# Last head takes up the former head's row sums at its first key pair; even heads' bound steps spread 2, 3, 2, 3

## Chip, cores and metric

One core of a Trainium2 chip runs the whole program in one launch. The metric is device time in microseconds (us), lower is better. The kernel before takes 1926.5 us, the median of three runs (1925.24 to 1927.55).

## What is computed

A layer norm without weights, attention of 32 heads against a given key and value cache, and a SwiGLU feed-forward whose activated output gates the attention's result:

```python
xn = layernorm(x)                                  # x: 2048 x 640, bf16
q  = (xn @ wq) in 32 heads of 192                  # wq: 640 x 6144
p  = softmax(q @ k_cache^T * 192**-0.5)            # 2048 keys for each head
s  = (p @ v_cache, heads joined) @ wo              # wo: 6144 x 640
g  = silu((silu(xn @ w1) * (xn @ w3)) @ w2)        # F = 1536
out = x + s * g
```

## The kernel before

The heads run one after the other. A head has four query blocks (`qb`) of 512 queries, and a block has eight key pairs (`p`, 0 to 7), each of two tiles of 128 keys. `step` (line 745) emits one pair: the scores matmuls of the pair into a PSUM tile `st` (L550, two such tiles exist, and the projection of the next head's queries takes its turn in them), the exponential on ACT (`weights`, L558) into the SBUF tile `pT`, and then some of the waiting value matmuls (`parts`), a few pairs behind the scores. At pair 1 of each block `extra` projects one block of queries of the next head (L355); in the last head, 31, it computes a piece of the feed-forward instead (`hidden_last`, whose two PSUM halves DVE casts to `gl` and `ul`, L952 and L953).

One `pT` tile holds two pairs, and the pool `pp` has three of them. So the tile that pairs 2 and 3 of a block write is the one that pairs 4 and 5 of the block before wrote.

Heads 2 to 30 (`in_quads`) multiply on 64x64 quarters of the array (L629), which leaves no room for a column of ones in the values, so DVE adds up the softmax's row sums (`row_sums`, all adds at L662): `fours` adds the two `pT` tiles of four pairs, twice in a block; `join` and `fold` add these up; `ends` makes the 128x512 tile `e` and has it turned by a DMA on SP's queue into `eT` (L688). `turned_sums` (L698 to L713, "the normalising" below) reduces `eT` to `rs`, takes the reciprocal, and scales the block's turned output `ox` into `ostage`. Before that `evict_quads` brings the block's output out of PSUM: ACT copies one half to `oa` (L653), DVE adds the other into `ot` (L654). Heads 0, 1 and 31 use 64x128 tiles with the ones column (L609) and need no such sums.

The sums are put off by a clock that counts pairs. `later(w, f)` lists a chore that is due `w` pairs on, and `do_chores` (line 720), the last act of each `step`, emits what is due. With the delays of the kernel the second `fours` of a block falls to pair 0 of the next block, `join`, `fold` and `ends` to its pair 2, and the normalising to pair 0 of the block after that. For head 30 the next blocks are those of head 31, and there `do_chores` returns at once at pairs 0 and 1.

`do_chores` also emits the list `lazy`: the steps by which an upper bound of the next head's scores is made, one at each pair in `slots`. Three key maxima (`fold_keys`, L407; the third also starts small copies on POOL), two sums of squares and the roots of them for the head's query weights (`column_lengths`, L428 and L434 to L442), and the bound itself (`head_bound`, DVE and one POOL reduction). An even head emits ten steps: seven for the next head, and the three of `column_lengths` for the head after that, which enter the list in the third block; an odd head emits four.

Nearly every instruction is pinned (`pin`): each engine takes its instructions in the order in which the program emits them. The tile framework adds the waits between engines and, for a tile of a pool, the wait for the last reader of the tile that had the space before.

Of the kernel before, what the change touches and what calls it, by code (L numbers as in the profile page):

```python
# [30 lines left out]
def _kernel_impl(ctx, tc, A_x, A_k_cache, A_v_cache, A_wq, A_wo, B_w1, B_w3, B_w2, out):  # L31
    nc = tc.nc
    _, SQ, D = A_x.shape
    _, H, SK, dh = A_k_cache.shape
# [5 lines left out]
    NQB = SQ // 512  # L40
# [109 lines left out]
    def in_quads(h):  # L150
        return 1 < h < H - 1
# [14 lines left out]
    with ExitStack() as actx:  # L166
# [491 lines left out]
        def later(wait, f, *a):  # L658
            chores.append((clock[0] + wait, f, a))

        def add(out, a, b):
            pin(nc.vector.tensor_tensor(out=out, in0=a, in1=b, op=ALU.add))  # L662

        def row_sums(hd, qb, p, w):
            sm = hd["sums"]

            def fours():
                t = aq["tree"].tile([P, 2, 1024], BF16, tag="tree", name="tree")
                a, b = sm["w"]
                sm["w"] = []  # L670
                add(t[:], a[:], b[:])
                sm["t"].append(t)

            def join():
                a, b = sm["t"]
                add(a[:], a[:], b[:])
                sm["t"].pop()

            def fold():
                t = sm["t"][0]  # L680
                add(t[:, 0, :], t[:, 0, :], t[:, 1, :])

            def ends():
                t = sm["t"].pop()[:, 0, :]
                e = aq["two"].tile([P, 512], BF16, tag="e", name="e")
                add(e[:], t[:, 0:512], t[:, 512:1024])
                eT = aq["two"].tile([P, 4, P], BF16, tag="eT", name="eT")
                pin(nc.sync.dma_start_transpose(out=eT[:], in_=e[:]))  # L688
                later(6, turned_sums, hd, qb, eT)

            sm["w"].append(w)
            if p % 4 == 3:
                later(2, fours)
            if p == NPAIR - 1:
                for f in (join, fold, ends):
                    later(4, f)
# [21 lines left out]
        aq = {}  # L718

        def do_chores(h, qb, p):  # L720
            if h == H - 1 and p < 2:
                return
            for c in [c for c in chores if c[0] <= clock[0]]:
                chores.remove(c)
                c[1](*c[2])
            slots = (5, 6, 7) if h % 2 == 0 or h == 1 else (5,)
            if p in slots and lazy and lazy[0][0] <= clock[0]:
                _, f, a = lazy.pop(0)
                f(*a)
# [15 lines left out]
        def step(hd, qb, p, extra=None):  # L745
            me = (hd["h"], qb)
            first = qb == 0 and p < 2
            st2 = scores(hd, qb, p, quads=before["quads"] if first else hd["quads"])
            old = [k for k, _ in parts if k != me]
            old_quads = bool(old) and heads_quads(old[0][0])  # L750
            if p == 1 and old_quads:
                while parts[0][0] != me:
                    next_part()
            pT2 = weights(st2, hd["nb"][qb], p)
            parts.extend((values_quads if hd["quads"] else values)(hd, qb, p, pT2))
            if hd["quads"] and p % 2 == 1:
                row_sums(hd, qb, p, acc["w"])
            if p == 0:
                while sum(k != me for k, _ in parts) > (2 if old_quads else 1):
                    next_part()  # L760
            elif p == 1:
                while parts[0][0] != me:
                    next_part()
            else:
                while len(parts) > (4 + (p > 2) if hd["quads"] else 3):
                    next_part()
            if extra:
                extra()
            while late:
                late.pop(0)()  # L770
            clock[0] += 1
            do_chores(hd["h"], qb, p)
# [129 lines left out]
        hx = fw.tile([P, SQ], BF16, name="hx")  # L902
        astack = ExitStack()
        fdp = astack.enter_context(tc.tile_pool(name="fdp", bufs=1, side="right"))
        for name, n in (("one", 1), ("two", 2), ("tree", 3)):
            aq[name] = astack.enter_context(tc.tile_pool(name=f"aq_{name}", bufs=n, side="right"))
        ffn_w_loads = [
            lambda: pin(nc.gpsimd.dma_start(out=w1_sb[:], in_=B_w1[:, FPIG + P:F].rearrange("(c p) f -> p c f", p=P))),
# [57 lines left out]
        for h in range(1, H):  # L966
# [10 lines left out]
            hd = heads[h]  # L977
# [11 lines left out]
            for qb in range(NQB):  # L989
                post = []  # L990
                if (h, qb) == (H - 1, 2):
                    while chores:
                        clock[0] += 1
                        do_chores(h, qb, 2)
                    astack.close()
                    acc["hTp"] = fstack.enter_context(tc.tile_pool(name="hTp", bufs=2, side="right"))
# [355 lines left out]
@with_exitstack  # L1352
def kernel(
    ctx: ExitStack,
    tc: tile.TileContext,
    A_x: bass.AP,
    A_k_cache: bass.AP,
    A_v_cache: bass.AP,
    A_wq: bass.AP,
    A_wo: bass.AP,  # L1360
    B_x: bass.AP,
    B_w1: bass.AP,
    B_w3: bass.AP,
    B_w2: bass.AP,
    out: bass.AP,
):
    _kernel_impl(ctx, tc, A_x, A_k_cache, A_v_cache, A_wq, A_wo, B_w1, B_w3, B_w2, out)
# [30 lines left out]
```

## Time and profile before

| | before |
|---|---|
| median of the runs | 1926.5 us (1925.24 to 1927.55) |
| the profiled execution | 1925.79 us |
| its span, first to last instruction | 1924.3 us |
| PE matmul busy | 1914.5 us (99%) |
| DVE, ACT, POOL busy | 1446.4 (75%), 1350.4 (70%), 600.3 us (31%) |
| granted TensorE clock, mean | 0.999 |

Times in the profile are microseconds from the first instruction of the profiled execution. A line of the timeline gives start, duration, engine, source line, operation, output<-inputs, and in brackets the idle time of the engine before it and what ended that. `xN` counts instructions merged into one line; the duration is then that of all. PE is the matmul unit, DVE the vector engine, ACT the scalar engine, POOL the general one, SP the one that starts most DMAs. Matmuls overlap, so the end of one lies after the start of the next.

### The profile page before, as it was taken

To read this page: it belongs to the slowest core of one execution; us is meant where nothing else is said; L and a number is where in the kernel's file an instruction comes from. 1 tells how busy PE (TensorE), PEld (TensorE's weight loads), DVE (VectorE), ACT (ScalarE), POOL (GpSimd) and SP (SyncE) were. 2 spreads that over 40 slices of the span, in tenths; PEclk is the share of its full clock that TensorE was granted. 3 is DMA by queue.
4 is the path that set the end of the run, shared out by engine and by line. 5 is a ranking of instruction groups with operands and counts; after the bars stand their busy time and mean duration, and the time that the engine had idled before them with its cause. 6 is when DMAs were issued, how large, how long until landed. Compare 5 with 4: busy or idle time off the path is not lost.

```text
span 1924.3 us, 75788 instructions
## 1 busy us (share of the span) xinstructions
PE 1914.5 (99%) x34631; PEld 1306.8 (68%) x34631; DVE 1446.4 (75%) x2326; ACT 1350.4 (70%) x1405; POOL 600.3 (31%) x757
## 2 busy tenths in 40 slices
PE   9999999999999999999999999999999999999999
PEld 5666667777777777777777777777777796454446
DVE  8668888888888888988888888888888875521111
ACT  7778888888888888888888888888888877210000
POOL 3433434343434333344333343433343320000000
PEclk9999999999999999999999999999999999999999
DMA  7714446444553455345544453446444523936763
GB/s 171 142 50 74 106 84 102 86 100 87 93 98 86 99 84 100 81 105 91 101 84 104 76 107 68 112 77 110 77 106 85 97 45 119 281 71 152 162 151 76
DMA packets 535684, 197.22 MB, mean 102 GB/s; under 512 B 486896, under 2 KB 528848, under 8 KB 535360
## 3 DMA queue, kind: packets, MB, share of 16 engines
q1 hardware_dynamic: 522416, 162.71, 43.5%
q0 software_dynamic: 8256, 24.58, 4.9%
q8 instruction: 271, 4.44, 1.0%
q10 hardware_dynamic: 4688, 5.05, 0.8%
q14 instruction: 53, 0.43, 0.1%
HBM read 54.26 MB, written 31.98 MB: 45 GB/s over the span
## 4 chain that ended last, share of the span: by engine, by line
PE 99%; SPq 0%; DVE 0%; ACT 0%; DMA 0%; POOL 0%; issue 0%; ACTq 0%
PE st L550 34%; PE obank L629 31%; PE ps L355 14%; PE ps_s L1142 8%; PE obank L609 3%; PE ps_s L1098 3%; PE ps_f L1162 2%; PE ps_gu L929 1%; PE ps_f L1178 1%; PE ps L340 0%; DMA KT<-in_A_k_cache_dram 0%; SPq L116 0%; PE ps_gu L340 0%; ACT pT L558 0%; SPq L100 0%; ACT xnT L283 0%
## 5 line engine op out<-in xcount | busy, mean ns | idle before, releaser
L558 ACT ACTIVATE pT<-st,nb 128x1024 bf16<-128x1024 f32 x1016 | 1124.6, 1113 | 182.0 <-PE st L550 151.6
L629 PE MATMUL obank<-pT,vt 64*64 64x256 bf16 (+1 forms) x14848 | 787.8, 323 | 0.0
L629 PEld LDWEIGHTS <-vt 64*64 64x64 bf16 x14848 | 499.7, 107 | 172.4 <-issue 1.9
L550 PE MATMUL st<-qS,KM 64*64 64x512 bf16 (+1 forms) x1951 | 416.7, 376 | 0.4 <-POOL qS L381 0.4
L550 PE MATMUL st<-qA,KT 64*64 64x512 bf16 (+1 forms) x1951 | 416.6, 376 | 0.0
L550 PE MATMUL st<-qD,KT 64*64 64x512 bf16 (+1 forms) x1951 | 416.6, 376 | 0.0
L550 PE MATMUL st<-qA,KM 64*64 64x512 bf16 (+1 forms) x1951 | 392.0, 376 | 0.0
L550 PE MATMUL st<-qS,KT 64*64 64x512 bf16 (+1 forms) x1951 | 391.9, 376 | 0.1
L550 PE MATMUL st<-qF,KT 64*64 64x512 bf16 (+1 forms) x1951 | 391.8, 376 | 0.0
L550 PEld LDWEIGHTS <-KT 64*64 64x64 bf16 (+1 forms) x7808 | 286.6, 107 | 129.8 <-issue 0.6
L381 POOL COPY qS<-qA 64x512 bf16<-64x512 bf16 x256 | 291.0, 1137 | 63.9 <-DVE qA L378 28.2
L662 DVE TENSOR_TENSOR tree<-pT,pT 128x2048 bf16<-128x2048 bf16 x232 | 299.7, 1292 | 1.6 <-ACT pT L558 1.6
L355 PE MATMUL ps<-xnT,wq 64*64 64x512 bf16 (+1 forms) x2390 | 291.8, 376 | 0.0
L355 PE MATMUL ps<-xnS,wq 64*64 64x512 bf16 (+1 forms) x2390 | 288.0, 376 | 0.0
L662 DVE TENSOR_TENSOR tree<-tree 128x2048 bf16<-128x2048 bf16 x232 | 265.8, 1146 | 4.0
L355 PEld LDWEIGHTS <-wq 64*64 64x64 bf16 (+1 forms) x4780 | 170.2, 107 | 74.7
L550 PEld LDWEIGHTS <-KM 64*64 64x64 bf16 (+1 forms) x3904 | 152.0, 106 | 54.8 <-issue 1.2
L385 POOL COPY qD<-qF 64x512 bf16<-64x512 bf16 x127 | 95.6, 753 | 292.1 <-ACT qF L378 288.2
L1142 PE MATMUL ps_s<-oT,wo_sb 128*128 128x512 bf16 x720 | 155.7, 379 | 0.0
L378 DVE CAST qA<-ps 128x512 bf16<-128x512 f32 x120 | 82.9, 691 | 95.2 <-ACT qF L378 94.6
L654 DVE TENSOR_TENSOR ot<-oa,obank 128x768 bf16<-128x768 f32 x116 | 110.1, 949 | 36.2 <-ACT oa L653 35.8
L653 ACT COPY oa<-obank 128x768 f32<-128x768 f32 x116 | 92.6, 798 | 62.8 <-PE obank L629 62.8
(159 smaller groups left out, 1628.8 us busy)
## 6 DMA issues: line engine op xcount, KB each, us to landing
o_scr<-ostage SPq DMA_DIRECT2D x64, 384.0 KB, 3.2
vt<-in_A_v_cache_dram SPq DMA_DIRECT2D x62, 384.0 KB, 4.9
wo_sb<-in_A_wo_dram POOLq DMA_DIRECT2D x1, 7680.0 KB, 30.6
wq<-in_A_wq_dram POOLq DMA_DIRECT2D x31, 160.0 KB, 4.2
hT_scr<-hblk SPq DMA_DIRECT2D x16, 256.0 KB, 2.9
xnS<-xnT POOLq DMA_DIRECT2D x8, 320.0 KB, 6.1
wq<-in_B_w_dram POOLq DMA_DIRECT2D x31, 80.0 KB, 3.7
wq<-in_A_wq_dram POOLq DMA_DIRECT2D x31, 80.0 KB, 3.3
```

The lines of the kernel that those rows point to most:

```text
L355: pin(nc.tensor.matmul(halves[t][c, :], lhsT=w[ROWS[t], s, c], rhs=xs[ROWS[t], s // 2, qs], start=(s == 0), stop=(s == 2 * DC - 1)))
L378: pin(c(out=dst[:, qs], in_=src))
L381: keep(nc.gpsimd.tensor_copy(out=qS[ROWS[t], qs], in_=qA[ROWS[1 - t], qs]))
L385: keep(copy(out=qD[:, qs], in_=qF[PGW:P, qs]))
L550: pin(nc.tensor.matmul(st2[c, t * 512:(t + 1) * 512], lhsT=k[:, c], rhs=q[ROWS[t], qs], start=(s == 0), stop=(s == 2)))
L558: pin(nc.scalar.activation(out=pT2, in_=st2[:], func=ACT.Exp, scale=SCALE, bias=nb[:]))
L609: pin(nc.tensor.matmul(acc["o"][b][:, r, (j % 2) * 256:(j % 2) * 256 + DH + 1], lhsT=pT2[ROWS[r], t * 512 + j * P:t * 512 + (j + 1) * P], ...
L629: pin(nc.tensor.matmul(acc["o"][r][ROWS[c], int(low), 0:n], lhsT=vt[ROWS[r], t, p, c0:c0 + DT], rhs=pT2[ROWS[r], t * 512 + q0:t * 512 + q0 ...
L653: pin(nc.scalar.copy(out=oa[:], in_=banks[0]))
L654: pin(nc.vector.tensor_tensor(out=ot[:], in0=oa[:], in1=banks[1], op=ALU.add))
L662: pin(nc.vector.tensor_tensor(out=out, in0=a, in1=b, op=ALU.add))
L1142: pin(nc.tensor.matmul(ps_of[d], lhsT=wo_sb[:, k, d * P:(d + 1) * P], rhs=part(k // KQ)[:, k % KQ, :], start=(k == 0), stop=(k == OC - 1)))
```

## The change

Three edits. In `do_chores` the last head no longer returns at pairs 0 and 1, so chores that are due there are emitted there. The normalising of head 30's last block gets a delay of 9 pairs in place of 6, and so falls to pair 3 of head 31's second block; it was at pair 2 of that block before, held up by the return. The slots of the even heads from 2 on are pairs 5 and 6 in the first and third block and 5, 6 and 7 in the second and fourth, where they were 5, 6 and 7 in all; since the list runs dry in the third block, where it was emitted 3, 3, 1, 3 it is now 2, 3, 2, 3. With that the third key maximum moves from the first block to the second, the roots from the second to the third, and the bound from pair 5 to pair 6 of the third block. The pool `tree` of the sums has two tiles in place of three.

```diff
                 pin(nc.sync.dma_start_transpose(out=eT[:], in_=e[:]))
-                later(6, turned_sums, hd, qb, eT)
+                later(6 if in_quads(hd["h"] + 1) or qb < NQB - 1 else 9, turned_sums, hd, qb, eT)
...
         def do_chores(h, qb, p):
-            if h == H - 1 and p < 2:
-                return
             for c in [c for c in chores if c[0] <= clock[0]]:
                 chores.remove(c)
                 c[1](*c[2])
-            slots = (5, 6, 7) if h % 2 == 0 or h == 1 else (5,)
+            slots = (5,) if h % 2 and h > 1 else (5, 6) if h > 1 and qb % 2 == 0 else (5, 6, 7)
...
-        for name, n in (("one", 1), ("two", 2), ("tree", 3)):
+        for name, n in (("one", 1), ("two", 2), ("tree", 2)):
```

## The prediction

> **What bounds the kernel now.** I read the page first, then who waited for whom, then the timelines of PE, ACT and DVE around PE's longest wait.
>
> ```profile
> span 1924.3 us, 75788 instructions
> ...
> PE 1914.5 (99%) x34631; PEld 1306.8 (68%) x34631; DVE 1446.4 (75%) x2326; ACT 1350.4 (70%) x1405; POOL 600.3 (31%) x757
> ...
> PE 99%; SPq 0%; DVE 0%; ACT 0%; DMA 0%; POOL 0%; issue 0%; ACTq 0%
> ```
>
> PE's matmuls are 99% of the span and of the chain that ended last. PE is without work for 1924.3 - 1914.5 = 9.8 us in all, and only there can a change of order gain. The view of waits says where (total, times, longest):
>
> ```profile
> PE obank L609 <- ACT pT L558: 3.1, 2, 2.9
> PE fill L217 <- DVE cols L182: 1.9, 1, 1.9
> PE st L550 <- POOL qS L381: 0.4, 1, 0.4
> PE ps L340 <- ACT xnT L283: 0.2, 1, 0.2
> ```
>
> The largest is one wait of 2.9 us for an exponential. PE's timeline places it at the start of head 31, where value matmuls are L609:
>
> ```profile
> 1584.34 0.38 PE L550 MATMUL st<-qF,KT 64*128 64x512 bf16 x1
> ...
> 1585.55 0.38 PE L550 MATMUL st<-qS,KM 64*128 64x512 bf16 x1
> ...
> 1586.20 0.50 PE L609 MATMUL obank<-vt,pT 64*128 64x193 bf16 x8
> 1589.58 0.51 PE L609 MATMUL obank<-vt,pT 64*128 64x193 bf16 x8 [2.88 <-ACT pT L558]
> 1589.92 0.38 PE L550 MATMUL st<-qS,KM 64*128 64x512 bf16 x1
> ...
> 1601.36 0.38 PE L550 MATMUL st<-qS,KM 64*128 64x512 bf16 x1
> ...
> 1602.67 0.38 PE L550 MATMUL st<-qS,KM 64*128 64x512 bf16 x1
> ```
>
> The first line ends the scores of pair 2 in head 31's first block, the second begins those of pair 3, the fifth those of pair 4: 1589.92 - 1585.55 = 4.37 us. The last two are the same pairs in its second block: 1602.67 - 1601.36 = 1.31 us. So the stall costs 4.37 - 1.31 = 3.06 us, a little more than the 2.88 of idle, since the last matmul's modelled tail counts as busy. ACT and DVE tell why:
>
> ```profile
> 1578.82 1.11 ACT L558 ACTIVATE pT<-st,nb 128x1024 bf16<-128x1024 f32 x1 [0.18 <-PE st L550]
> ...
> 1583.54 1.14 ACT L524 ACTIVATE pt<-qF 64x512 bf16<-64x512 bf16 x2
> 1588.41 2.12 ACT L558 ACTIVATE pT<-st,nb 128x1024 bf16<-128x1024 f32 x2 [3.73 <-DVE tree L662]
> ```
>
> ```profile
> 1575.60 1.21 DVE L662 TENSOR_TENSOR tree<-pT,pT 128x2048 bf16<-128x2048 bf16 x1
> 1582.67 0.95 DVE L654 TENSOR_TENSOR ot<-oa,obank 128x768 bf16<-128x768 f32 x1 [5.86 <-ACT oa L653]
> 1584.01 0.69 DVE L952 CAST gl<-ps 128x512 bf16<-128x512 f32 x1 [0.38 <-PE ps L355]
> 1584.61 0.68 DVE L953 CAST ul<-ps 128x512 bf16<-128x512 f32 x1
> 1585.21 0.68 DVE L702 TENSOR_REDUCE rs<-eT 128x4 f32<-128x512 bf16 x1
> ...
> 1587.08 1.22 DVE L662 TENSOR_TENSOR tree<-pT,pT 128x2048 bf16<-128x2048 bf16 x1
> ```
>
> The exponential of pair 2 (ACT, 1588.41) waits 3.73 us for a row-sum add. It writes the `pT` tile that pairs 4 and 5 of head 30's last block filled, and the add at 1587.08, the second `fours` of that block, is that tile's last reader. The early return holds `fours` until pair 2, and in front of it the normalising of head 30's third block (from 1585.21). Meanwhile DVE had stood idle for 5.86 us, from 1576.81 to 1582.67.
>
> **The chores at pair 0.** The normalising of block 3 and `fours` now come ahead of `ot` on DVE, into that idle time. The normalising needs the turned tile `eT`; for this one, then for all 116 of them:
>
> ```profile
> L688 SPq DMA_TRANSPOSE eT<-e x1: 2192/2192/2192, 1575.7 to 1575.7; - x1
> ...
> DMA to landing us min/median/max: 3.3/3.3/3.3
> ```
>
> ```profile
> DMA to landing us min/median/max: 2.4/3.3/4.8
> ```
>
> It lands at 1575.7 + 3.3 = 1579.0. The normalising takes 1587.08 - 1585.21 = 1.87 us and ends at 1580.87. `fours` also needs the exponential of head 30's pair 7, which ended at 1578.82 + 1.11 = 1579.93, so it starts at 1580.87 and ends at 1582.09. That is 0.58 us ahead of `ot` at 1582.67, which waits for ACT's copy as before. So `ot` and the casts stay where they are, and the wait of 3.73 us is gone: by 1584.68 (1583.54 + 1.14) ACT is through its two tanh, at 1584.72 (1584.34 + 0.38) the scores of pair 2 are done, and with 1.11 us the exponential runs to about 1585.9. PE wants its result behind the eight matmuls from 1586.20; eight take 0.34 us (1589.58 to 1589.92), so at 1586.54, with some 0.6 us to spare. Gain: the whole 3.06 us.
>
> The unknown is when `eT` lands, because these instructions now stand before `ot` and the casts, for which PE waits: `ot` frees the output bank, and `ul` the PSUM tile of pair 3's scores. At the slowest landing seen, 4.8 us, the chain is 1580.5 + 1.87 + 1.22 (`fours`) + 0.95 (`ot`) + 0.60 (from `gl` to `ul`) + 0.68 = 1585.82, against 1584.61 + 0.68 = 1585.29 now. The scores of pair 3 began at 1585.55, 0.26 us behind the cast, so 0.53 - 0.26 = 0.27 us would be lost. An earlier landing gains nothing more. The bounds of this edit are therefore 2.79 and 3.06 us; I take 3.06, since the 3.3 us is the row of this very transfer.
>
> Nothing else comes due next. `join`, `fold` and `ends` stay at pair 2 with no reader that PE waits for. What follows head 31 hangs on PE's own progress and moves up with it.
>
> **The normalising put off.** Four DVE instructions (1.87 us) move from pair 2 to pair 3 of head 31's second block. DVE's next deadline there is the output of that block:
>
> ```profile
> 1609.45 0.56 DVE L581 COPY osum<-obank 128x386 f32<-128x386 f32 x1 [2.55 <-PE obank L609]
> ```
>
> With 2.55 us idle ahead of it, the move costs nothing; without that cover a pair, 1.31 us, would be the most.
>
> **Two tree tiles.** `join` and `ends` give both tiles back at pair 2, and the next `fours` takes one at pair 4. Writers and readers are all on DVE, which runs in order, so no engine can wait for a tile that it would have had: 0 on both sides.
>
> **The spread.** Head 8 shows all four blocks: first the starts of the projections (the last column counts matmuls), then DVE, then POOL.
>
> ```profile
> 427.36 2.16 PE ps L355 x40
> 439.89 2.16 PE ps L355 x40
> 452.43 2.16 PE ps L355 x40
> 465.19 2.16 PE ps L355 x40
> ```
>
> ```profile
> 434.83 3.46 DVE L407 TENSOR_REDUCE mk<-KT 128x1 f32<-128x1024 bf16 x3
> ...
> 447.37 0.81 DVE L428 SCALAR_TENSOR_TENSOR wt<-wt 128x640 bf16<-128x640 bf16 x1
> ...
> 450.26 0.17 DVE L442 TENSOR_SCALAR ln<-ln 128x2 f32<-128x2 f32 x1
> ...
> 459.53 1.62 DVE L662 TENSOR_TENSOR tree<-pT,pT 128x2048 bf16<-128x2048 bf16 x1
> ...
> 462.08 0.69 DVE L702 TENSOR_REDUCE rs<-eT 128x4 f32<-128x512 bf16 x1 [0.48 <-DMA eT<-e]
> ...
> 466.06 0.95 DVE L654 TENSOR_TENSOR ot<-oa,obank 128x768 bf16<-128x768 f32 x1 [0.89 <-ACT oa L653]
> ```
>
> ```profile
> 458.25 1.81 POOL L381 COPY qS<-qA 64x512 bf16<-64x512 bf16 x2
> ```
>
> A block takes 12.53 to 12.54 us of PE with three maxima (3.46 us of DVE) or with squares and roots (447.37 to 450.43, 3.06 us): three steps in a block cost PE nothing already. The first block loses 3.46 / 3 = 1.15 us of DVE, the second swaps roots for a maximum, and the third gets the roots. These are at most 3.06 - 2 x 0.81 = 1.44 us, against 0.48 us of waiting for `eT` and 0.89 us of waiting for ACT, 1.37 in all, behind them. What is left over, 0.07 us, falls on work that PE does not wait for at once. I take 0; for a bound, 15 even heads at 0.07 us are 1.1 us lost.
>
> The third block took 465.19 - 452.43 = 12.76 us, 0.22 too many. Its tree add lasted 1.62 us, not 1.21, beside POOL's copies (458.25 to 460.06), and the exponential of pair 6 waited for it; the view of waits puts all of these on the instruction behind the add:
>
> ```profile
> ACT pT L558 <- DVE km L466: 4.2, 7, 0.7
> ```
>
> Seven such waits at 0.22 us bound what all of them cost PE: 1.5 us. The edit does not aim at the add, which stays at pair 4, ahead of the bound steps, so I count nothing.
>
> **The sum.** 1925.79 (a span of 1924.3 and 1.49 around it) - 3.06 = 1922.73 us. The profiled execution lies 0.71 us below the median of the runs, so the forecast for a median is 1926.5 - 3.06 = 1923.4 us, 0.16% less. About 0.2%, 3.85 us, is what a measurement of this kernel can tell from no change.
>
> **Rivals.**
>
> *More is gained.* If the altered order of DVE and POOL also clears the seven waits in the even heads, up to 1.5 us come on top: 1926.5 - 3.06 - 1.5 = 1921.9 us. For it: a first block lighter by 1.15 us. Against it: the slow add and POOL's copies lie ahead of the moved steps. Chance 0.12.
>
> *The stall moves or stays.* Either `eT` lands late, which leaves a gain of 2.79 us and less, or the exponential has a second thing to wait for that the row does not name; with the stall kept whole it is 1926.5 us. For it: the chain through `ot` and the casts has only 0.58 + 0.26 us of play. Against it: ACT's row names the add alone, and the scores and casts it also needs are there. Chance 0.12, middle 1925.
>
> *Slower: tree adds fall on POOL's copies in more blocks.* The third maximum's POOL copies move to the second block and the bound's POOL reduction by a pair, so POOL's other copies can shift onto the adds. Price 0.22 us a block, as in head 8; over 3.06 / 0.22 = 14 newly hit blocks it decides. All 15 even heads hit in three blocks would be 45 x 0.22 - 3.06 = 6.8 us slower, 1933.3. Against it: the moved POOL work is small, and 116 blocks show seven such waits. Chance 0.08.
>
> [...]
>
> **How the numbers follow.** The forecast keeps 0.68: 1923.4 us. The runs of before lie 1.26 us below to 1.05 above their median, so its own range is about 1922.3 to 1924.8. With the middle of the second rival and most of the first, the range is 1921.9 to 1925.4 us; outside lie the slower rival and the ends of the others. A measured gain over 3.85 us needs the first rival (0.12) or scatter of 0.8 us the right way, some 0.12 of the forecast's 0.68: faster 0.24. Slower is the third rival, 0.08. Within 0.2%: 0.68.
>
> **What would show it.** In the profile after, the wait of PE's L609 for ACT is down to some tenths; the row sums' add `tree<-pT,pT` stands before `ot` in head 31, starting 1.87 us after `rs`; pairs 3 to 4 take 1.31 us; PE's busy time stays at 1914.5 us and the span falls to about 1921.3. I would be wrong if ACT's exponential of pair 2 still waits, if PE waits at pair 3 for `ul`, or if even heads' blocks leave 12.54 us.

## Result and profile after

The changed kernel takes 1923.07 us (median of 20 runs, 1922.48 to 1924.14) against 1926.67 for the kernel before (20 runs, 1925.24 to 1927.98). The ratio is 0.9982, with a 95% interval of 0.9975 to 0.9988: 3.6 us, 0.18%. The forecast was 1923.4, which is 0.3 us more. Three single runs of the experiments below (3397 and 8127 us with a fourth `pT` tile, and 7236 us of the kernel before) lie far outside all others and are left out of the ratios.

The page and the view of waits of the profiled execution after (1922.95 us; waits are total, times, longest):

```profile
span 1921.4 us, 75765 instructions
...
PE 1912.8 (100%) x34608; PEld 1299.3 (68%) x34631; DVE 1447.3 (75%) x2326; ACT 1350.4 (70%) x1405; POOL 599.5 (31%) x757
```

```profile
ACT pT L558 <- DVE ss L434: 4.6, 7, 0.7
...
PE fill L217 <- DVE cols L182: 1.9, 1, 1.9
...
PE st L550 <- POOL qS L381: 0.8, 1, 0.8
...
PE obank L609 <- ACT pT L558: 0.2, 1, 0.2
```

PE's wait for the exponential is down from 3.1 us to 0.2. (PE's busy time is 1.7 us lower although its work is the same; 23 matmul records are missing here, 34608 beside 34631 weight loads.) PE, ACT and DVE at the start of head 31:

```profile
1586.15 0.38 PE L550 MATMUL st<-qS,KM 64*128 64x512 bf16 x1
...
1586.80 0.83 PE L609 MATMUL obank<-vt,pT 64*128 64x193 bf16 x16
1587.47 0.38 PE L550 MATMUL st<-qS,KM 64*128 64x512 bf16 x1
```

```profile
1584.15 1.14 ACT L524 ACTIVATE pt<-qF 64x512 bf16<-64x512 bf16 x2
1585.36 1.11 ACT L558 ACTIVATE pT<-st,nb 128x1024 bf16<-128x1024 f32 x1
```

```profile
1579.25 0.69 DVE L702 TENSOR_REDUCE rs<-eT 128x4 f32<-128x512 bf16 x1 [1.84 <-DMA eT<-e]
...
1581.13 1.22 DVE L662 TENSOR_TENSOR tree<-pT,pT 128x2048 bf16<-128x2048 bf16 x1
1583.27 0.95 DVE L654 TENSOR_TENSOR ot<-oa,obank 128x768 bf16<-128x768 f32 x1 [0.92 <-ACT oa L653]
```

The first line begins the scores of pair 3, the last those of pair 4. Pairs 3 to 4 now take 1587.47 - 1586.15 = 1.32 us, where it was 4.37. The normalising and the add stand in DVE's idle time ahead of `ot`, which still waits 0.92 us for ACT, and the exponential of pair 2 follows the tanh without a DVE wait.

### The profile page after: what moved, and what is told of

Read it like the earlier page. It is cut to its first block, busy times and chain, and to the rows that moved or that the text cites. A ratio compares the mean times of both kernels' runs of the same rounds, so it can differ in the third digit from the quotient of the medians.

```text
span 1921.4 us, 75765 instructions
## 1 busy us (share of the span) xinstructions
PE 1912.8 (100%) x34608; PEld 1299.3 (68%) x34631; DVE 1447.3 (75%) x2326; ACT 1350.4 (70%) x1405; POOL 599.5 (31%) x757
## 4 chain that ended last, share of the span: by engine, by line
PE 99%; DVE 0%; ACT 0%; DMA 0%; issue 0%; POOL 0%
PE st L550 34%; PE obank L629 31%; PE ps L355 14%; PE ps_s L1140 8%; PE obank L609 3%; PE ps_s L1096 3%; PE ps_f L1160 2%; PE ps_gu L927 1%; PE ps_f L1176 1%; PE ps L340 0%; DVE st L400 0%; DMA x_all<-in_A_x_dram 0%; DVE st L225 0%; PE ps_gu L340 0%; ACT xnT L283 0%
```

## Experiments

Each kernel was compared with runs of the kernel before on the same chip, whose medians there were 1926.8 to 1926.96 us.

**1. The return alone, against the kernel before.**

```diff
-            if h == H - 1 and p < 2:
-                return
```

> Only the early return of the last head is removed; the normalising of head 30's last block keeps its delay of 6 pairs and so comes at pair 0 of head 31's second block, the spread and the pool of tree tiles are as before. Theory (the whole gain is the stall of pair 2): 3.06 us less than before, about 1923.5, PE's long wait for the exponential gone. If the normalising at pair 0 holds up the output adds behind it, up to 1.87 us of this is lost again at the start of the second block, 1925.4. Rival (the spread gives part of the gain): clearly less than the 3.6 us by which the changed kernel won.

1923.85 us, ratio 0.9986 (0.9977 to 0.9995). The old stall is gone and a smaller one is new, in head 31's second block:

```profile
1596.88 0.33 PE L609 MATMUL obank<-vt,pT 64*128 64x193 bf16 x4
1598.24 1.01 PE L609 MATMUL obank<-vt,pT 64*128 64x193 bf16 x20 [1.03 <-DVE osum L582]
1599.44 0.37 PE L550 MATMUL st<-qS,KM 64*128 64x512 bf16 x1 [0.19 <-DVE ul L951]
```

```profile
1595.17 0.68 DVE L702 TENSOR_REDUCE rs<-eT 128x4 f32<-128x512 bf16 x1
...
1597.04 0.55 DVE L581 COPY osum<-obank 128x386 f32<-128x386 f32 x1
1597.63 0.56 DVE L582 TENSOR_TENSOR osum<-osum,obank 128x386 f32<-128x386 f32 x1
```

With a delay of 6 the normalising (1595.17 to 1597.04) comes between the two output banks that DVE has to empty, and PE waits 1.03 + 0.19 us for the second bank and for `ul`. From the scores of pair 2 to those of pair 3 it takes 1599.44 - 1596.24 = 3.20 us, where the kernel before takes 1601.36 - 1599.71 = 1.65: 1.55 us are lost. That is what the delay of 9 avoids. The median lies between the two that were expected, 1923.5 without such a loss and 1925.4 with 1.87 us of it.

**2. The return and the delay** (the changed kernel with the old slots and three tree tiles).

> The changed kernel without the spread and with three tree tiles: the early return removed and the normalising put off. Theory (the spread and the tree pool are worth nothing): as the changed kernel, a median of 1923.1 within 0.4 us, every run's granted clock at 1.000, head 31's first block at 12.86 us. Against the kernel that only lost the return, the loss at the start of head 31's second block (1.4 us in its trace, waits of PE for osum and ul) is gone. Rival (the spread carries the 0.5 us by which the gain exceeded 3.06): a median of 1923.6 or more.

1922.46 us, ratio 0.9978 (0.9969 to 0.9987). PE waits neither for `osum` nor for `ul`. All of the gain is here; that it is 0.6 us more than expected is within the interval, and experiment 7 compares this order with the changed kernel on one chip.

**3. The spread alone, against the kernel before.**

```diff
-            slots = (5, 6, 7) if h % 2 == 0 or h == 1 else (5,)
+            slots = (5,) if h % 2 and h > 1 else (5, 6) if h > 1 and qb % 2 == 0 else (5, 6, 7)
```

> Only the slots of the even heads are changed (2, 3, 2, 3). Theory: no change, 0 to 0.2 us, the stall of 2.9 us at the start of head 31 still there, and again about seven short waits of the exponential in the even heads' third blocks. Rival (more is gained by the spread): 0.5 to 1.5 us less and fewer of the short waits.

1927.65 us, ratio 1.0003 (0.9995 to 1.0012), with the short waits again:

```profile
ACT pT L558 <- DVE ss L434: 5.3, 8, 0.8
...
ACT pT L558 <- DVE tree L662: 3.7, 1, 3.7
```

The spread gains nothing. But this profile brought something new. PE around the old stall, then windows of this execution and, in the third view, of the kernel before. (A window's line gives its start and end, its length, the busy time and the number of instructions of PE, of its weight loads, of DVE, ACT and POOL, and then the granted clock, DMA share and GB/s.)

```profile
1586.96 0.38 PE L550 MATMUL st<-qS,KM 64*128 64x512 bf16 x1
...
1587.61 0.50 PE L609 MATMUL obank<-vt,pT 64*128 64x193 bf16 x8
1590.99 0.83 PE L609 MATMUL obank<-vt,pT 64*128 64x193 bf16 x8 [2.88 <-ACT pT L558]
1591.61 0.63 PE L550 MATMUL st<-qS,KM 64*128 64x512 bf16 x1
...
1592.89 1.19 PE L609 MATMUL obank<-vt,pT 64*128 64x193 bf16 x16
1593.92 0.38 PE L550 MATMUL st<-qS,KM 64*128 64x512 bf16 x1
```

```profile
1588.00:1590.00 2.00, 0.11 (x4) 0.00 (x0) 1.97 (x4) 0.18 (x1) 0.00 (x0) 1.00 0.00 0
1590.00:1592.00 2.00, 1.01 (x10) 0.73 (x12) 1.93 (x3) 2.00 (x3) 0.00 (x0) 0.55 0.00 0
1592.00:1594.00 2.00, 2.00 (x24) 1.36 (x22) 1.93 (x5) 1.26 (x2) 0.00 (x0) 0.59 0.32 62
1594.00:1596.00 2.00, 2.00 (x34) 1.28 (x32) 1.28 (x3) 1.43 (x2) 0.00 (x0) 1.00 0.06 11
```

```profile
1588.00:1590.00 2.00, 0.42 (x10) 0.42 (x12) 1.93 (x3) 1.59 (x2) 0.00 (x0) 1.00 0.00 0
1590.00:1592.00 2.00, 2.00 (x35) 1.29 (x32) 1.93 (x5) 2.00 (x3) 0.00 (x0) 1.00 0.01 2
...
1920.00:1924.00 4.00, 0.15 (x3) 0.00 (x0) 0.58 (x2) 0.00 (x0) 0.00 (x0) 0.77 0.13 31
```

The idle time is the same 2.88 us as before, but here the mean granted clock is 0.55 and 0.59 in two windows, 1590 to 1594, with 1.00 in those on both sides, and a scores matmul takes 0.63 us, not 0.38. In the last whole microsecond of the kernel before, 1923 to 1924 without a matmul, the clock is 0.50. If it is the same here, the two means stand for 0.45 x 2 / 0.5 = 1.80 and 0.41 x 2 / 0.5 = 1.64 us, from about 1590.2 to 1593.6, an estimate. By it the clock falls some 2.1 us after the end of PE's last matmul (1587.61 + 0.50), while PE still stands idle. Pairs 3 to 4 take 4.65 us and pairs 4 to 5 2.31, together 1.28 more than 4.37 and 1.31. In the profiled execution of the kernel before, the windows around the stall show a clock of 1.00.

The mean clock of each run hints at how often it happens. Of 34 runs of the kernel before, 11 have 1.000 (median 1925.58 us, none over 1926.06) and 23 have 0.999 or less (median 1927.41, none under 1926.48). In the two later comparisons 10 of 31 and 8 of 23 have 1.000, and the medians of the two groups lie 1.40 and 1.77 us apart. All 20 runs of the changed kernel have 1.000. A fall as long as this one takes 0.0009 off the mean (0.45 x 2 + 0.41 x 2 = 1.72 us of 1926.6), so a mean of 1.000 rules it out; a mean of 0.999 does not prove it, because the time after PE's last matmul counts too. The profiled execution of the kernel before has its 0.999 from there alone (the last line above). The stall would then cost more than its 3.06 us, in some runs. Two kernels test that.

**4. The same stall with PE kept at work**, against the kernel before (inside `step`):

```diff
             st2 = scores(hd, qb, p, quads=before["quads"] if first else hd["quads"])
+            for _ in range(4 if (hd["h"], qb, p) == (H - 1, 0, 3) else 0):
+                scores(hd, qb, p, st2=st2)
```

> The kernel before, in which PE computes the scores of pair 3 of head 31's first block five times in place of once, so that it works through most of the time in which it stood still (the same values are written again; 24 matmuls more). The stall of 3.06 us stays, with about 0.4 us of it idle. Theory (beside its own 3.06 us the stall makes the clock fall in two of three runs, which costs these about 1.3 to 2 us more): all runs at a clock of 1.000 and at 1924.6 to 1926.1 us, median about 1925.6, 1.0 to 1.4 us less than before although more is computed. Rival (the two groups of runs of the kernel before have another cause): again two groups, median 1927, some clocks at 0.999.

```profile
1584.61 0.38 PE L550 MATMUL st<-qS,KM 64*128 64x512 bf16 x1
...
1587.85 0.50 PE L609 MATMUL obank<-vt,pT 64*128 64x193 bf16 x8
1588.64 0.51 PE L609 MATMUL obank<-vt,pT 64*128 64x193 bf16 x8 [0.29 <-ACT pT L558]
1588.99 0.38 PE L550 MATMUL st<-qS,KM 64*128 64x512 bf16 x1
```

Pairs 3 to 4 take 1588.99 - 1584.61 = 4.38 us, as before, but only 0.29 us of it is idle. All 11 runs have a clock of 1.000 and lie at 1923.98 to 1925.45 us; the median is 1925.08 against 1926.94, ratio 0.9991 (0.9982 to 1.0). With 24 matmuls more the kernel is 1.9 us faster, 0.5 us more than expected. Not all of this is the clock: the runs of before that have 1.000 in this comparison have a median of 1925.74 us, 0.66 above this kernel's. Its profiled execution lost 0.3 us in the even heads' blocks, that of the kernel before 1.1.

**5. The stall shortened**, against the kernel before:

```diff
-            for c in [c for c in chores if c[0] <= clock[0]]:
+            due = [c for c in chores if c[0] <= clock[0]]
+            if h == H - 1 and qb == 0:
+                due.sort(key=lambda c: c[1].__name__ != "fours")
+            for c in due:
```

> The kernel before, in which at pair 2 of head 31 the row sums' add is emitted ahead of the normalising. Theory (the stall is set by what stands in front of the add on DVE): the exponential starts 1.87 us earlier, PE's idle time falls from 2.88 to about 1.0 us, 1.87 us less, and with the shorter idle no run's clock falls: 1923.7 us, 3.2 us less than the median of before. Rival (idle of any length there makes the clock fall): 1.9 us less than before with clocks of 0.999 among the runs.

```profile
1585.84 0.38 PE L550 MATMUL st<-qS,KM 64*128 64x512 bf16 x1
...
1586.49 0.50 PE L609 MATMUL obank<-vt,pT 64*128 64x193 bf16 x8
1588.00 0.51 PE L609 MATMUL obank<-vt,pT 64*128 64x193 bf16 x8 [1.02 <-ACT pT L558]
1588.35 0.38 PE L550 MATMUL st<-qS,KM 64*128 64x512 bf16 x1
```

Pairs 3 to 4 take 2.51 us, 1.86 less, as worked out. All 11 runs have a clock of 1.000; the median is 1924.27, ratio 0.9988 (0.9979 to 0.9997), 0.6 us above what was expected. The profiled execution lost 1.6 us in the even heads' blocks, where that of the kernel before lost 1.1, which may be part of it.

**6. A fourth `pT` tile**, in the kernel before and in the changed one (two tree tiles in both):

```diff
-        pp = actx.enter_context(tc.tile_pool(name="pp", bufs=3))
+        pp = actx.enter_context(tc.tile_pool(name="pp", bufs=4))
```

> The kernel before with four pT tiles in place of three (and two tree tiles, for the space). The order of the instructions is as before, with the row sums' add at pair 2 of head 31. Theory (the exponential waits only because the add is the last reader of the tile it writes): the stall goes without any reordering, 2.9 to 3.06 us less; and the seven short waits in the even heads go too, since they are the same kind of wait, about 1.1 us more: 1922.5. Rival (the exponential or PE waits for DVE at that place for another reason): the stall stays, 1926.6.

> The changed kernel with four pT tiles in place of three. Theory: the seven short waits go, 1.1 us less than the changed kernel, 1922.0, about 4.2 us less than before; the blocks of heads 4, 8, 12, 16, 24 and 28 that take 12.67 to 12.77 us fall to 12.54. Rival (these blocks lose their time to something else than the wait for the tile): as the changed kernel, 3.1 to 3.6 us less than before.

1922.05 us, ratio 0.9977 (0.9968 to 0.9985), and 1922.01 us, ratio 0.9976 (0.9967 to 0.9986). In the first, DVE's order is that of before, with the add after the casts, and the stall is 0.26 us, one pair later:

```profile
1585.94 1.22 DVE L662 TENSOR_TENSOR tree<-pT,pT 128x2048 bf16<-128x2048 bf16 x1
```

```profile
1587.69 0.50 PE L609 MATMUL obank<-vt,pT 64*128 64x193 bf16 x8
1588.44 0.51 PE L609 MATMUL obank<-vt,pT 64*128 64x193 bf16 x8 [0.26 <-ACT pT L558]
```

So the stall was the wait for a tile and nothing else.

**7. The fourth tile with the two edits that gain** (experiment 2 with four `pT` and two tree tiles), run twice, the second time beside the changed kernel with and without the spread:

> The changed kernel's first two edits (return removed, normalising put off) with four pT tiles, two tree tiles and the slots of before. Theory: no wait for a pT tile is left, neither at the start of head 31 nor in the even heads, 12.54 us in all blocks of heads 2 to 30 but one or two: 1921.9 us. The kernel before with four pT tiles alone lost 0.35 us more in head 31's first block than this would; so 0.1 to 0.4 us less than it, if their starts are alike. Rival (the four pT tiles made the runs of 3397 and 8127 us among those of the changed kernel with four): such runs here too.

> The changed kernel once more, to stand beside the next kernel on one chip. Theory (the spread is worth nothing): the two agree within 0.2 us. Rival (the spread costs something in the even heads' third blocks): this one is 0.4 to 0.7 us slower than the next.

> The changed kernel with the slots of before, all else as changed, two tree tiles included. Theory (spread and tree pool are worth nothing): as the changed kernel beside it within 0.2 us. Rival (the spread costs something): 0.4 to 0.7 us faster than the changed kernel, as the three pairs with and without the spread that ran apart from each other suggest (1927.65 against 1926.96, 1923.07 against 1922.46, 1922.01 against 1921.50).

> Return removed, normalising put off, slots of before, four pT tiles, two tree tiles: the kernel without the spread with a fourth pT tile. Theory (the short waits of the even heads are waits for a pT tile): faster than the kernel without the spread on the same chip by the 0.7 to 1.1 us that the blocks of the even heads lose. Rival (they only move): no difference.

| on one chip | median us | ratio to before (95%) |
|---|---|---|
| changed kernel | 1922.87 | 0.9979 (0.9970 to 0.9988) |
| without the spread | 1922.77 | 0.9978 (0.9969 to 0.9987) |
| without the spread, four `pT` tiles | 1921.53 | 0.9975 (0.9965 to 0.9986) |

The first comparison gave 1921.50, ratio 0.9973 (0.9963 to 0.9983). The spread is worth 0.1 us, no difference; the 0.4 to 0.7 us that comparisons on different chips had suggested does not hold. The fourth tile is worth 1.24 us here (medians of 8 runs with it and 11 without) and 0.96 us in the first comparison, where experiment 2 took 1922.46. Head 8 in the last kernel's profile, projections and DVE:

```profile
451.92 2.16 PE ps L355 x40
...
464.46 2.16 PE ps L355 x40
```

```profile
458.90 1.62 DVE L662 TENSOR_TENSOR tree<-pT,pT 128x2048 bf16<-128x2048 bf16 x1
```

The third block takes 12.54 us, not 12.76, although the add still lasts 1.62 us. This kernel has the lowest median of the three.

## Why the prediction was right, point by point

- **The stall and its cause.** Right. The exponential waited for the last reader of its `pT` tile (experiments 1 and 6), and what stood ahead of that reader on DVE set the length (experiment 5: 1.86 us less for 1.87 us moved).
- **The chain at pair 0.** Right. `eT` landed 2.9 us after its issue, `rs` began at 1579.25, the add 1.88 us later, and `ot` had 0.92 us to spare where I had 0.58. Nothing was lost at pair 3.
- **The price of the stall.** Too small, by a term that was missing. The step "the stall costs 4.37 - 1.31 = 3.06 us" holds for the profiled execution, whose clock stayed up at the stall. I carried 3.06 over to the median of the runs. That the profiled execution lay 0.71 us below this median was noted and not asked about: in it, as in at least 29 of the 88 runs (mean clock 1.000), the clock did not fall there. In others the same stall costs more, 1.28 us in the one trace that shows the fall and 1.4 to 1.8 us by the groups of runs. Experiments 4 and 5 left 0.29 and 1.02 us of idle time, and all 22 runs have a mean clock of 1.000.
- **How near the number came.** This is in part luck. In the first comparison the median of before lies 1926.96 - 1925.58 = 1.38 us above that of its full-clock runs, so by the account above the stall should be worth about 3.06 + 1.38 = 4.4 us of median, an estimate. Measured were 3.6, with an interval of 2.3 to 4.8, and 3.9 in experiment 7 (without the spread 4.5 in experiment 2 and 4.0 in experiment 7). The difference of 0.5 to 0.8 us is not explained; the even heads' blocks differ by as much between traces (0.3 us lost in experiment 4, 1.1 before, 1.6 in experiment 5).
- **The normalising put off.** Right that it costs nothing. What I did not work out is the alternative: the return removed and the delay left at 6 cost 1.55 us at the start of head 31's second block (experiment 1).
- **Two tree tiles.** Priced at 0, and nothing contradicts it: the kernels of experiment 2 and of the table's second row differ in this alone, and each has a ratio of 0.9978, though on different chips. The space of the third tree tile is that of the fourth `pT` tile.
- **The spread.** Right at 0, by the means stated: in head 8 the roots used up what `rs` had waited for `eT`, and `ot` kept 0.19 us of its wait.
- **The seven short waits.** Their bound, 1.5 us, was about right: the fourth tile, which removes them, gained 0.96 and 1.24. They are still seven in the changed kernel, so the rival "more is gained" did not come in. They are waits for a `pT` tile like the large one.
- **The slower rival.** It did not come in, 7 waits before and 7 after. The add beside POOL's copies in head 8 took 1.62 us before and 1.61 after (458.55 to 460.37 are the copies there), where the median of all 232 is 1.22 in both traces and the longest 1.64. In head 8 of experiment 7 the add takes 1.62 us too, and at 12.54 us the block loses nothing once the exponential has a free tile.

## What to carry to other kernels

When an engine waits for a tile of a rotating pool, look for the tile's last reader and for what its engine does ahead of it: the reader can move forward, or the pool can have one tile more, and the second also catches the waits that are too short to stand out. Ask why a profiled execution is faster than the median of its runs before carrying its durations over to them, and compare the granted clocks of the runs and where in a trace the clock falls, since the mean also counts the time after the last matmul (0.77 from 1920 to 1924 us in the kernel before, with 0.15 us of matmuls). Variants that differ by half a microsecond in two thousand have to run on one chip in one comparison: apart, the spread seemed to cost 0.4 to 0.7 us, and on one chip it was 0.1.

## What was not expected of the hardware

Two traces show a single stall of PE with 2.88 us idle. In that of experiment 3 the mean granted clock is 0.55 and 0.59 in the windows from 1590 to 1594, in that of the kernel before 1.00 in all windows around the stall. By the runs of the kernel before, at most 59 of 88 saw such a fall: so many have a mean clock of 0.999 or less (23 of 34, 21 of 31, 15 of 23). With 1.02 us idle (experiment 5), or 0.29 (experiment 4), all 11 runs each have 1.000.

What decides between the two outcomes, and how much idle time between 1.02 and 2.88 us it takes, is not shown by these runs.
